# Forty more squared score tiles, 58 pre-added row sums and a tabled instruction order in a two-part attention kernel

## The chip, the cores and the metric

The kernel runs on one core of a Trainium2 chip. The metric is device time in microseconds of one execution; three executions of the kernel before took 1046.61, 1047.0 and 1047.89 us, so their median is 1047.0. The names used below: PE is TensorE (matmuls; its weight loads are shown as PEld), ACT is ScalarE, DVE is VectorE, POOL is GpSimd, SP is SyncE, which here only issues transfers. Line numbers are those of the kernel before unless a line is said to be of the changed one, where the same code lies some 40 to 100 lines further down.

## What is computed

Two attention layers over 2048 tokens of width 1024, with 32 heads of 32 numbers each, whose outputs are laid side by side. Part A is plain softmax attention. Part B cuts the sequence into four segments of 512 tokens, does causal softmax attention inside each, and mixes it with a running memory of the earlier segments.

```python
def _A_ref(x, wqkv, wo):
    qkv = (x @ wqkv).reshape(B, S, 3, H, Dh).transpose(2, 0, 3, 1, 4)
    scores = jnp.einsum('bhqd,bhkd->bhqk', qkv[0], qkv[1]) * Dh ** (-0.5)
    o = jnp.einsum('bhqk,bhkd->bhqd', softmax(scores), qkv[2])
    return o.transpose(0, 2, 1, 3).reshape(B, S, D) @ wo
...
        for s in range(N):                      # part B, segment by segment
            p = _softmax(einsum('bhqd,bhkd->bhqk', qs, ks) * scale + mask)
            a_dot = jnp.einsum('bhqk,bhkd->bhqd', p, vs)
            num = jnp.einsum('bhld,bhde->bhle', phi(qs), M)
            den = jnp.einsum('bhld,bhd->bhl', phi(qs), z)[..., None] + 1e-06
            outs.append(g * num / den + (1.0 - g) * a_dot)
            M = M + jnp.einsum('bhld,bhle->bhde', phi(ks), vs)
            z = z + jnp.einsum('bhld->bhd', phi(ks))
...
    return jnp.concatenate([a, b], axis=-1)
```

## The kernel before

**Tiles and sets.** Heads go in groups of four (`g`, eight groups), queries in chunks of 256 (`c`, eight chunks). A pair `("A", g, c)` is a unit of part A: 64 units. A unit goes over its 2048 keys in eight sets, numbered 0 to 7 by their place in the unit. A set is 256 keys (two key blocks of 128) against the chunk's 256 queries for four heads: four tiles of 128 partitions by 512 columns, one per head, the two key blocks side by side. `plan_set` issues a set's scores as one run of eight matmuls (line 1271, "score row" below) into four PSUM banks. Six banks form three slots of two banks (`SLOT_BANKS`), which the sets use in turn, so that a score row can only go when the exponentials two and three places before it in ACT's stream have emptied their banks. The remaining two banks (`POOL_BANKS`) are shared by the accumulators and all other matmul work. Part B adds 80 sets of the same kind, cut to the causal shape; there are 592 sets in all.

**Exponentials.** For each set ACT runs two instructions (line 1347), each over two tiles: 128x1024, from PSUM to the bf16 tile `P`, a ring of 20 buffers of 512 columns.

**Squared tiles.** In some sets of part A the first of the four tiles isn't exponentiated: DVE writes `Y = a*s + b` (line 1308) and POOL multiplies `Y` by itself into `Pc` (line 1311), a parabola that stands for the exponential of these small scores; a constant that is missing is added through `job_corr` (line 1481) and `cu` (line 1504). The set's first exponential then covers one tile only, 128x512. `SQUARES` names, for each head group, the places in a unit whose sets have such a tile; `Y` has three buffers and `Pc` four. The last two units, ("A", 7, 6) and ("A", 7, 7), and the early units of group 0 have none.

**Products.** `round` (lines 1438 and 1445) does a set's second half: for each of the two key blocks four matmuls of 256 columns with the values `V`, and four with ones, which give the row sums for the softmax. The four matmuls of a group lie in four column strips of the array and run side by side. All of a unit's products add up in one bank; `norm` reads it after the last.

**Jobs.** Everything else (projections at line 899, evictions on DVE at line 1658, output products, memory updates, squares of K and Q at line 1672 that guard the exponential's range) is cut into jobs that are slipped between score rows.

**What sets the order.** The planner makes a list of operations with a duration, a key and due times. `schedule` was a list scheduler: engine by engine it took the ready operation with the best rank, out of constants such as `AHEAD`, `STICK` and `JOB_SLOPE`, and a table `SHIFT` of many hundred numbers moved single operations' keys. After it every engine has a fixed sequence of instructions with waits on the other engines' counters; an engine that waits holds up all that stands behind it.

Of the kernel before, what the change touches and what calls it, by code (L numbers as in the profile page):

```python
# [11 lines left out]
P = 128  # L12
H = 32
DH = 32
S = 2048
# [9 lines left out]
OL_LEAD, OL_MAX = 3.567283411686441, 21.60561264796846  # L25
# [8 lines left out]
SQUARES = ((1, 3, 4, 6, 7), (1, 3, 4, 6, 7), (1, 3, 4, 6), (1, 3, 5, 7), (1, 3, 5, 7), (1, 3, 5, 7), (1, 3, 5, 7), (1, 4, 6))  # L34
HOST = 2
CORR_AT = -0.496
# [3 lines left out]
SOON = 0.5969023125738563  # L40
# [88 lines left out]
class Op:  # L129
# [4 lines left out]
    def __init__(self, eng, fn, dur, lat, key, mode=None, sem=None):  # L134
# [16 lines left out]
SWITCH = 0.1  # L151
WIN = 3.413
ROW_LEAD = 5.053495059459838
AHEAD = 1.6055122421540051
HEAT = 8.05297032017043
STICK = 3.256770423473878
OVER = 17.394741454160474
PV_ROOM = 6.408007584666841
PV_T = 1.0806361081944706
PV_HOT = 1.0883878031673944  # L160
NORM_K = 6.738
JOB_AT = 1.5887710826754966
JOB_SLOPE = 1.1413237083257293
# [3 lines left out]
LEAD_A, LEAD_B, DUE_AT, DUE_SLOPE = 10.658, 3.249, 7.018517831572489, 1.9480960937294671  # L167
HOLD = {}
BACKLOG = 3.378
XR = 70.3728830950375  # L170
XC = 5.80397040345515
# [4 lines left out]
SAFE = 0.0  # L176
SHIFT = {((f, n), e): v for f, e, t in (
# [10 lines left out]
    ("plan_constants", "ACT", {  # L188
        1: 15.5}),
    ("plan_constants", "POOL", {  # L190
        0: 5.5, 2: 4.25, 3: -3, 4: 10.25, 6: -9.5, 7: -0.75, 8: -0.75, 9: 2.25, 11: 3.25, 12: -7, 13: 3.75, 14: -12.25,
        15: 2.5, 16: -0.5, 17: -4.75, 18: 1.5, 19: 3.25, 20: -0.5, 21: 15, 23: 0.75}),
    ("plan_exp", "POOL", {
# [10 lines left out]
    ("plan_jobs", "ACT", {  # L204
# [4 lines left out]
    ("plan_jobs", "DVE", {  # L209
# [91 lines left out]
    ("plan_prologue", "ACT", {  # L301
        4: 6, 5: 3.75, 8: 4, 10: 10}),
    ("plan_prologue", "DVE", {
        0: -2.25, 5: 6, 6: 8.25, 7: -3, 9: -8.5, 10: 0.5}),
    ("plan_prologue", "PE", {
        2: 1.5, 5: -3.25, 6: 12, 7: 5, 8: 17.25, 9: 0.5}),
# [2072 lines left out]
```

## Time and profile before

| | |
|---|---|
| median of three executions | 1047.0 us |
| span of the profiled execution (first to last instruction) | 1044.3 us |
| its own time | only its span is shown; the median is 2.7 us above it |
| granted TensorE clock | 1.000 |
| PE, busy share of the span | 98% |
| ACT | 97% |
| DVE | 67% |
| POOL | 56% |

A matmul's end is modelled and matmuls overlap in the pipeline, so PE's 98% says only that something was under way; how much room PE has is read from what its weight loads wait for, and from the distance between starts. The same holds on ACT, where an instruction begins before the one ahead of it has ended. A row of the groups shows count, busy time, the mean duration of one, the idle time before them and what ended it; a row of the waits shows the time waited in total, how often, and the longest.

### The profile page before, as it was taken

To read this page: it belongs to the slowest core of one execution; us is meant where nothing else is said; L and a number is where in the kernel's file an instruction comes from. 1 tells how busy PE (TensorE), PEld (TensorE's weight loads), DVE (VectorE), ACT (ScalarE), POOL (GpSimd) and SP (SyncE) were. 2 spreads that over 40 slices of the span, in tenths; PEclk is the share of its full clock that TensorE was granted. 3 is DMA by queue.
4 is the path that set the end of the run, shared out by engine and by line. 5 is a ranking of instruction groups with operands and counts; after the bars stand their busy time and mean duration, and the time that the engine had idled before them with its cause. 6 is when DMAs were issued, how large, how long until landed. Compare 5 with 4: busy or idle time off the path is not lost.

```text
span 1044.3 us, 56017 instructions
## 1 busy us (share of the span) xinstructions
PE 1019.2 (98%) x25384; PEld 559.9 (54%) x25385; DVE 700.4 (67%) x1559; ACT 1016.3 (97%) x1225; POOL 585.5 (56%) x677
## 2 busy tenths in 40 slices
PE   8999999999999999999999999999999999999998
PEld 4555555655555555565555545565555545455554
DVE  3366676767566686887865687687755885874444
ACT  5999989999999999999999999999999999999997
POOL 2125476668645675766656476665644775653310
PEclk9999999999999999999999999999999999999999
DMA  9042352124313331033223320133113561021101
GB/s 210 15 96 54 78 130 36 20 38 106 80 42 92 80 79 34 11 99 51 71 58 94 98 60 18 28 92 54 51 29 87 174 171 25 24 79 57 59 24 59
DMA packets 171390, 72.17 MB, mean 69 GB/s; under 512 B 134800, under 2 KB 169360, under 8 KB 171152
## 3 DMA queue, kind: packets, MB, share of 16 engines
q1 hardware_dynamic: 168784, 67.79, 26.7%
q8 instruction: 200, 3.28, 1.3%
q10 hardware_dynamic: 2368, 0.79, 0.3%
q14 instruction: 38, 0.31, 0.1%
HBM read 45.29 MB, written 11.73 MB: 55 GB/s over the span
## 4 chain that ended last, share of the span: by engine, by line
PE 66%; ACT 29%; DVE 3%; issue 1%; DMA 1%; POOL 0%; ACTq 0%; DVEq 0%
PE ps L899 32%; ACT P L1347 28%; PE ps L1271 13%; PE ps L1438 9%; PE ps L1445 9%; PE ps L1964 1%; DMA xT_A<-in_A_x_dram 1%; ACT PKQ_B L2008 1%; DVE Y L1308 1%; DVE T L1508 0%; PE ps L1715 0%; DVE OT_B L2035 0%; DVE T L1510 0%; DVE KQ_B L1658 0%; PE ps L1814 0%
## 5 line engine op out<-in xcount | busy, mean ns | idle before, releaser
L1347 ACT ACTIVATE P<-ps 128x1024 bf16<-128x1024 f32 (+1 forms) x1176 | 988.4, 1059 | 9.8 <-PE ps L1271 3.2
L1311 POOL TENSOR_TENSOR Pc<-Y 128x512 bf16<-128x512 f32 x238 | 249.4, 1049 | 257.2 <-PE ps L899 79.3
L1445 PE MATMUL ps<-P,onesb 128*32 128x256 bf16 (+1 forms) x4388 | 295.9, 270 | 0.8 <-issue 0.7
L1438 PE MATMUL ps<-P,V_A 128*32 128x256 bf16 x3620 | 252.7, 274 | 0.4 <-DVE V_A L1974 0.3
L1308 DVE TENSOR_SCALAR Y<-ps 128x512 f32<-128x512 f32 x238 | 163.4, 686 | 97.7 <-PE ps L1271 83.8
L1271 PE MATMUL ps<-KQ_A 32*128 32x256 bf16 x4096 | 204.0, 273 | 7.4 <-ACT P L1347 5.7
L1271 PEld LDWEIGHTS ps<-KQ_A 32*128 32x128 bf16 x4096 | 62.0, 92 | 154.0 <-ACT P L1347 111.7
L1445 PEld LDWEIGHTS ps<-P,onesb 128*32 128x32 bf16 x4388 | 128.8, 96 | 25.9 <-issue 12.9
L899 PE MATMUL ps<-xT_A,W_A 128*32 128x512 bf16 (+1 forms) x2236 | 138.8, 363 | 2.3 <-DMA xT_A<-in_A_x_dram 1.2
L899 PE MATMUL ps<-xT_B,W_B 128*32 128x512 bf16 (+1 forms) x2284 | 139.0, 359 | 1.2 <-DVE KQ_B L1658 0.3
L1438 PEld LDWEIGHTS ps<-P,V_A 128*32 128x32 bf16 x3620 | 107.7, 96 | 26.2 <-issue 10.9
L1438 PE MATMUL ps<-Pc,V_A 128*32 128x256 bf16 x476 | 119.5, 273 | 0.2
L1445 PE MATMUL ps<-Pc,onesb 128*32 128x256 bf16 x476 | 119.6, 274 | 0.0
L1370 POOL TENSOR_SCALAR_AFFINE_SELECT P<-P 128x768 bf16<-128x768 bf16 (+1 forms) x96 | 75.7, 794 | 49.9 <-ACT P L1347 48.3
L1672 POOL TENSOR_TENSOR sqA<-KQ_A 128x512 bf16<-128x512 bf16 x61 | 64.0, 1061 | 60.9 <-PE ps L899 31.5
L1672 POOL TENSOR_TENSOR sqB<-KQ_B 128x512 bf16<-128x512 bf16 x64 | 68.4, 1070 | 24.9 <-DVE KQ_B L1658 19.0
L899 PEld LDWEIGHTS ps<-xT_B,W_B 128*32 128x32 bf16 x2284 | 53.2, 96 | 46.6 <-issue 17.1
L899 PEld LDWEIGHTS ps<-xT_A,W_A 128*32 128x32 bf16 x2236 | 52.0, 96 | 48.7 <-issue 17.1
L1521 DVE STREAM_TRANSPOSE T<-rc 128x256 f32<-128x256 f32 (+1 forms) x152 | 72.3, 479 | 2.6
L899 PE MATMUL ps<-Wv_B,xT_B 128*32 128x512 bf16 (+1 forms) x1124 | 71.0, 362 | 0.8 <-issue 0.7
L1658 DVE CAST KQ_B<-ps 128x512 bf16<-128x512 f32 x64 | 44.1, 688 | 39.1 <-PE ps L899 38.4
L899 PE MATMUL ps<-Wo_B,OT_B 128*32 128x512 bf16 (+1 forms) x1112 | 68.6, 364 | 0.3 <-DVE T L1504 0.2
(117 smaller groups left out, 1224.5 us busy)
## 6 DMA issues: line engine op xcount, KB each, us to landing
Wv_B<-in_B_wv_dram SPq DMA_DIRECT2D x32, 256.0 KB, 3.3
W_B<-in_B_wk_dram SPq DMA_DIRECT2D x32, 256.0 KB, 3.4
W_B<-in_B_wq_dram SPq DMA_DIRECT2D x32, 256.0 KB, 4.0
Wo_B<-in_B_wo_dram SPq DMA_DIRECT2D x32, 256.0 KB, 3.3
out_dram<-outsb SPq DMA_DIRECT2D x56, 128.0 KB, 1.9
W_A<-in_A_wqkv_dram SPq DMA_DIRECT2D x14, 256.0 KB, 3.4
ot_a_scratch<-OTst SPq DMA_DIRECT2D x51, 64.0 KB, 1.8
xT_A<-ot_a_scratch SPq DMA_DIRECT2D x6, 512.0 KB, 4.9
```

Source lines behind the costliest of these rows:

```text
L899: ins = e.matmul(out[r], w[:, r], x, start=start, stop=stop, tile_position=(0, 32 * t), skip_group_check=True)
L1271: ins = e.matmul(out, kap, qap, start=st, stop=True, tile_position=(32 * h, 0), skip_group_check=True)
L1308: o = self.dve(lambda e: e.tensor_scalar(Y[:, :], src, KAPPA * SCALE, BETA, ALU.mult, ALU.add), 512, key - 9.0, [self.bank[bank]], [rY], f ...
L1311: last.append(self.pool(lambda e: e.tensor_tensor(dst, Y[:, :], Y[:, :], ALU.mult), 512, key - BCK, [rY], [rP], rate=0.56))
L1347: a = self.act(guarded if early else lambda e: e.activation(dst, src, ACT.Exp, scale=SCALE), cols, key, rd, wr, fixed=EXP_FIXED + (0.095 i ...
L1370: self.pool(lambda e: e.affine_select(v, v, pattern=pat, compare_op=ALU.is_ge, fill=0.0, base=0, channel_multiplier=-1), 2 * nd * P, key + ...
L1438: ins = e.matmul(self.pb(obk, q0, q0 + nq, slice(32 * h, 32 * h + 32)), v, p, start=first, stop=last, tile_position=(0, 32 * h), skip_grou ...
L1445: ins = e.matmul(self.pb(obk, QC + q0, QC + q0 + nq, slice(32 * h, 32 * h + 32)), self.onesb[:, 0:32], p, start=False, stop=last, tile_pos ...
L1521: self.dve(lambda e: e.transpose(L2.rearrange("p (b r) -> p b r", r=32), bc), n, key, [rr], [rl], fixed=0.17)
L1658: self.dve(lambda e: e.tensor_copy(dst, src()), 512, key, [self.at(b)], rdst, fixed=0.155)
L1672: self.pool(lambda e: e.tensor_tensor(sq[:, :], src, src, ALU.mult), 512, key, [rsrc], [rs], rate=0.56)
L1964: o = self.pe(lambda e, i=i, t=t, k=k: e.matmul(self.pb(b, P * k, P * k + P), self.xT[:, i, P * t:P * t + P], self.WAv[:, i, P * half:P * ...
```

## The change

It has three parts, and two smaller ones.

First, `SQUARES` gives the places 1, 3, 4, 6, 7 to the head groups 2 to 6 too, which had four of them. That is one more squared tile in each of 40 units: 278 tiles where there were 238.

Second, in 58 units of part A one set that has no squared tile gets its row sums in another way (`ADDED`, `plan_add`, `sums`). POOL adds the set's two key blocks for all four heads into a tile `S` (one instruction, 128x1024 bf16 out of twice as many), and four matmuls with ones take `S`, in place of the eight that took the two blocks. `S` has one buffer.

Third, the list scheduler's choice is gone. `ORDER` holds, for each engine, runs of operations by their place in the planner's list, and `schedule` replays them; the constants of the ranks and `SHIFT` are gone with it.

The smaller ones: `load_xB` brings a segment of part B's input in four transposing transfers of 128x2x512 in place of one of 128x8x512, so 16 in place of 4 over the program; and `BACKLOG`, which spaces out transfers, is 1.2 in place of 3.378.

```diff
-SQUARES = ((1, 3, 4, 6, 7), (1, 3, 4, 6, 7), (1, 3, 4, 6), (1, 3, 5, 7), (1, 3, 5, 7), (1, 3, 5, 7), (1, 3, 5, 7), (1, 4, 6))
+SQUARES = ((1, 3, 4, 6, 7), (1, 3, 4, 6, 7), (1, 3, 4, 6, 7), (1, 3, 4, 6, 7), (1, 3, 4, 6, 7), (1, 3, 4, 6, 7), (1, 3, 4, 6, 7), (1, 4, 6))
+ADDED = (((0, 2, 5), 1, 'POOL'), ((0, 2, 5), 1, 'POOL'), ... ((0, 2, 3, 5, 7), 1, 'POOL'))
+S_RING = 1
+ADDED_PV = 5.0
-BACKLOG = 3.378
+BACKLOG = 1.2
-SHIFT = {((f, n), e): v for f, e, t in (
...
+ORDER = {
...
+        queue = {}
+        for e, runs in ORDER.items():
+            at, q = 0, []
+            for jump, n in zip(runs[::2], runs[1::2]):
+                at += jump
+                q += self.ops[at:at + n]
+                at += n
...
+    def plan_add(self, take, buf, eng, T):
+        i = self.nS % S_RING
+        self.nS += 1
+        rS = self.r_S[i]
+        take[0]["S"] = (i, rS)
+
+        def f(key):
+            lo, hi = self.Pt[:, buf:buf + 4, 0:QC], self.Pt[:, buf:buf + 4, QC:2 * QC]
+            fn = lambda e: e.tensor_tensor(self.S[:, i, :, :], lo, hi, ALU.add)
...
+                self.pool(fn, 4 * QC, key, self.r_P[buf:buf + 4], [rS], rate=0.56)
...
+    def sums(self, t, n, take, key):
+        ob = t["ol"]
+        i, rS = take[0]["S"]
+
+        def mm(e):
+            for h in range(4):
+                ins = e.matmul(self.pb(ob.grp, QC, 2 * QC, slice(32 * h, 32 * h + 32)), self.onesb[:, 0:32], self.S[:, i, h, :],
+                               start=False, stop=True, tile_position=(0, 32 * h), skip_group_check=True)
...
-            for mm in (mm_o, mm_l):
+            for mm in (mm_o, mm_l) if "S" not in parts[0][0][0] else (mm_o,):
...
-        self.turn(self.xTB[:, :, :], xb[L * s:L * s + L, :], self.sm_xTB, key, [], [self.r_xTB], 5.0, 3.4, True)
+        self.pieces(key, X_STEP, [lambda e, i=i: e.dma_start(self.xTB[:, i:i + 2, :], src[:, P * i:P * i + 2 * P], transpose=True)
+                                  for i in range(0, 8, 2)], self.sm_xTB, [self.r_xTB], ("x", s), 3.4, issue=1.25, svc=2.0)
```

What this moves is shown at three places, before and after each. The first is ACT's sequence in the middle of the program (head group 3), where `128x1024` is an exponential of two tiles and `128x512` one beside a squared tile. Before:

```order
L1347 ACTIVATE P<-ps 128x1024 x3
L1347 ACTIVATE P<-ps 128x512
L1347 ACTIVATE P<-ps 128x1024 x3
L1347 ACTIVATE P<-ps 128x512
L1347 ACTIVATE P<-ps 128x1024 x3
```

and now:

```order
L1424 ACTIVATE P<-ps 128x1024 x3
L1424 ACTIVATE P<-ps 128x512
L1424 ACTIVATE P<-ps 128x1024
L1424 ACTIVATE P<-ps 128x512
L1424 ACTIVATE P<-ps 128x1024 x3
```

Every second set had a short exponential; now two neighbouring sets have one, then one set has none.

The second place is PE at the first products of a unit of head group 3: `KQ_A` is a score row, `P,V_A` and `P,onesb` are the products of a key block of four heads with values and with ones, `Pc` is the squared tile among them, `Wv_A,xT_A` a projection, `S` the added blocks. Before:

```order
L1445 MATMUL ps<-P,onesb 32x256 x4
L1438 MATMUL ps<-Pc,V_A 32x256
L1438 MATMUL ps<-P,V_A 32x256 x3
L1445 MATMUL ps<-Pc,onesb 32x256
L1445 MATMUL ps<-P,onesb 32x256 x3
L1271 MATMUL ps<-KQ_A 128x256 x8
```

and now, in the changed kernel's line numbers:

```order
L937 MATMUL ps<-Wv_A,xT_A 32x256 x40
L1534 MATMUL ps<-P,V_A 32x256 x12
L1541 MATMUL ps<-P,onesb 32x256 x4
L1346 MATMUL ps<-KQ_A 128x256 x8
L1534 MATMUL ps<-P,V_A 32x256 x4
L1541 MATMUL ps<-P,onesb 32x256 x4
```

Twelve products with values now stand in a row where a product with ones stood between each two: the two products with ones of the added set are gone there. They come back as one group, after the score row that follows:

```order
L1541 MATMUL ps<-Pc,onesb 32x256
L1541 MATMUL ps<-P,onesb 32x256 x3
L1495 MATMUL ps<-S,onesb 32x256 x4
L1534 MATMUL ps<-Pc,V_A 32x256
L1534 MATMUL ps<-P,V_A 32x256 x3
```

The third place is POOL, just behind a memory update of part B (`Mb`), where squares of scores (`Pc`), squares of K and Q (`sqA`) and a unit's scaled output (`OTst`) follow one another. Before:

```order
L2075 TENSOR_TENSOR Mb<-Mf,maskbd 128x256
L1672 TENSOR_TENSOR sqA<-KQ_A 128x512
L1311 TENSOR_TENSOR Pc<-Y 128x512 x3
L1570 TENSOR_TENSOR OTst<-T_0 128x256
L1311 TENSOR_TENSOR Pc<-Y 128x512 x2
```

and now:

```order
L2171 TENSOR_TENSOR Mb<-Mf,maskbd 128x256
L1288 TENSOR_TENSOR S<-P 128x1024
L1388 TENSOR_TENSOR Pc<-Y 128x512 x2
L1680 TENSOR_TENSOR T_1<-T_1 128x256
L1681 TENSOR_TENSOR OT_B<-T_1,OT_B 128x256
```

The add of a whole set stands ahead of squares, which POOL takes up only when it is done.

More of the change, by code (lines that the diff above doesn't have):

```diff
@@ L509, in schedule @@
     def schedule(self):
-        pend = {}
-        groups = list(dict.fromkeys(o.grp for o in self.ops if o.grp is not None))
-        for g in groups:
-            own = {*g.pe, *g.rd}
-            first = g.pe[0]
-            g.left = len(g.pe)
-            if g.chain:
-                continue
-            first.gate = [(x, 0.0) for o in g.pe[1:] for x in (o.deps | o.order) - own]
-            first.gate += [(x, sum(o.dur for o in g.pe)) for o in g.rd for x in (o.deps | o.order) - own]
-            assert g.rd and not any(x.grp is g and x not in own for x in first.deps)
@@ L549, in schedule @@
+        for q in queue.values():
+            for n, o in enumerate(q):
+                o.pos = n
+        for o in self.ops:
+            assert all(x.eng != o.eng or x.pos < o.pos for x in o.order)
+        at = dict.fromkeys(queue, 0)
+        free = dict.fromkeys(queue, 0.0)
+        ready = dict.fromkeys(queue)
         last = {b: list(r.w) + list(r.r) for b, r in self.before.items()}
         holder = dict.fromkeys(last)
-        st = self.st = dict(mode=None, prog=0.0, act_end=0.0, recent=[], win=0, acts={}, slow=0.0, opn=0, dma=0.0,
-                            rows=sum(o.urgent is not None and o.eng == "PE" for o in self.ops))
+        acts, win, low, mode, held, dma = {}, 0, False, None, 0.0, 0.0
@@ L554, in ready_of @@
+        done = set()
+        progs, was_pe = [], None
+        for g in dict.fromkeys(o.grp for o in self.ops if o.grp is not None):
+            g.left = len(g.pe)
         def ready_of(o):
             t = 0.0
-            job = SAFE if o.eng == "PE" and o.urgent is None else 0.0
+            for x in o.deps | o.order:
+                if x not in done:
+                    return None
             for x in o.deps:
-                t = max(t, x.end + (SELF if x.eng == o.eng and x.sem is None else x.lat) + (job if x.eng in ("DVE", "POOL") else 0.0) +
+                t = max(t, x.end + (SELF if x.eng == o.eng and x.sem is None else x.lat) +
@@ L559, in ready_of @@
                         (TO_POOL if o.eng == "POOL" and x.eng == "DVE" else 0.0) +
                         (TO_DVE if o.eng == "DVE" and x.eng == "PE" else 0.0))
-            for x in o.order:
-                t = max(t, x.start)
-            for x, w in o.gate:
-                t = max(t, x.end + x.lat - w)
-            return t
-        def past(t):
-            return next((x for x in reversed(queue["ACT"]) if x.prog and x.end <= t), None)
-        def opens(o):
-            return o.grp is not None and o is o.grp.pe[0]
@@ L574, in opening @@
-        def opening(o, now=False):
-            g = o.grp
-            if g.sums and ((g.prev is not None and (g.prev.left or not all(x.sched for x in g.prev.rd))) or st["opn"] < g.at and st["rows"] and not now):
-                return 1e9, None
-            return min((1e9 if holder[b] is not None and holder[b].left else
-                        max((x.end + x.lat + SAFE if x.sched else 1e9 for x in last[b]), default=0.0), b) for b in last)
-        def heat(t, span):
-            r = st["recent"]
-            while r and r[0][1] < t - 4.0:
-                r.pop(0)
-            return sum((min(e, t) - max(s, t - span)) * w for s, e, w in r if e > t - span)
@@ L635, in schedule, with opening @@
+            return max([t] + [x.start for x in o.order])
+        def opening(b):
+            if holder[b] is not None and holder[b].left or not done.issuperset(last[b]):
+                return 1e9
+            return max((x.end + x.lat for x in last[b]), default=0.0)
+        left = len(self.ops)
         while left:
             best = None
-            for e, c in cand.items():
-                if c:
-                    t = max(free[e], min(x.ready for x in c))
-                    if best is None or t < best[0]:
-                        best = (t, e)
@@ new lines, in schedule @@
+            for e, q in queue.items():
+                if at[e] == len(q):
+                    continue
+                o = q[at[e]]
+                if ready[e] is None:
+                    ready[e] = ready_of(o)
+                    if ready[e] is None:
+                        continue
+                t, b = max(free[e], ready[e]), None
+                if o.grp is not None and o is o.grp.pe[0]:
+                    v, b = min((opening(b), b) for b in last)
+                    if v >= 1e9:
+                        continue
+                    t = max(t, v)
+                if e == "SP" and o.svc >= 0.8:
+                    t = max(t, dma - BACKLOG)
+                if best is None or t < best[0]:
+                    best = (t, e, o, b)
@@ L1009, in alloc @@
         self.p_n = 0
+        self.S = sb("S", [P, S_RING, 4, QC])
+        self.r_S = [Res() for _ in range(S_RING)]
+        self.nS = 0
+        self.nadd = {}
         self.Y = [sb(f"Y{i}", [P, 512], dt.float32) for i in range(Y_RING)]
@@ L1224, in squared, with added @@
         return SQUARES[unit[1]]
+    def added(self, unit, part, at):
+        if unit[0] != "A" or part is not None or unit in WHOLE:
+            return None
+        ats, most, eng = ADDED[unit[1]]
+        if at not in ats or self.nadd.get(unit, 0) == most or self.p_n % P_RING + 4 > P_RING:
+            return None
+        self.nadd[unit] = self.nadd.get(unit, 0) + 1
+        return eng
+    def plan_add(self, take, buf, eng, T):
[6 more added lines that the diff above has]
+            fn = lambda e: e.tensor_tensor(self.S[:, i, :, :], lo, hi, ALU.add)
+            if eng == "DVE":
+                self.dve(fn, 4 * QC, key, self.r_P[buf:buf + 4], [rS], rate=1.92, fixed=0.155, port=True)
+            else:
+                self.pool(fn, 4 * QC, key, self.r_P[buf:buf + 4], [rS], rate=0.56)
+        self.item(T + 0.05, f, take[0]["set"])
     def plan_set(self, take, T):
@@ L1234, in plan_set @@
         cube = kind == "A" and at in self.squared(take[0]["unit"], take[0]["part"])
-        bufs = [self.p_next(2 - (cube and not k)) for k in range(2)]
+        add = self.added(take[0]["unit"], take[0]["part"], at) if kind == "A" else None
+        assert add is None or not cube
+        if add is not None:
+            bufs = [self.p_next(4)]
+            bufs.append(bufs[0] + 2)
+        else:
+            bufs = [self.p_next(2 - (cube and not k)) for k in range(2)]
         for k, t in enumerate(take):
@@ L1284, in plan_set @@
             T += (2 - lo) * w / 1200.0 + EXP_FIXED
+        if add is not None:
+            self.plan_add(take, bufs[0], add, T)
         u = take[0]["unit"]
```

239 lines of the change are left out of this document (60 added, 179 removed), and 673 rows, old and new, of tables (ORDER, SHIFT).

## The prediction

> **What bounds the kernel now.** I read the page first, then who waits for whom, then the gaps between starts, then the stretches of the program.
>
> ```profile
> span 1044.3 us, 56017 instructions
> PE 1019.2 (98%) x25384; PEld 559.9 (54%) x25385; DVE 700.4 (67%) x1559; ACT 1016.3 (97%) x1225; POOL 585.5 (56%) x677
> PEclk9999999999999999999999999999999999999999
> ```
>
> Two engines look full and two have room; the clock is granted in full throughout, so no time is to be had there. Which of the two full ones leads is told by the waits of all engines; a row has waiter, what it waits for, total, times, longest:
>
> ```profile
> PEld ps L1271 <- ACT P L1347: 133.8, 416, 1.5
> PEld ps L1271 <- DVE Y L1308: 21.5, 67, 0.6
> PEld ps L1271 <- issue: 14.7, 62, 0.4
> ACT P L1347 <- PE ps L1271: 3.2, 8, 0.9
> ```
>
> PE's score rows wait for exponentials 416 times; ACT is seen waiting for score rows 8 times. So ACT leads. How much room does PE have? A row that waits for nothing still shows about 0.24 us (14.7 over 62, "issue"); the timeline around such a row shows 0.21 us between the last group ahead and the row:
>
> ```profile
> 500.03 0.27 PE L1445 MATMUL ps<-Pc,onesb 128*32 128x256 bf16 x1
> 500.14 0.27 PE L1438 MATMUL ps<-Pc,V_A 128*32 128x256 bf16 x1
> 500.25 0.27 PE L1445 MATMUL ps<-Pc,onesb 128*32 128x256 bf16 x1
> 500.46 0.40 PE L1271 MATMUL ps<-KQ_A 32*128 32x256 bf16 x8
> ```
>
> Taking 0.21 off each of the 416 + 67 waits leaves 155.3 - 101.4 = 54 us: PE's true room is some 54 us, 5% of the span, not the 2% of the page.
>
> ACT isn't as full as it looks either. Its instructions overlap, so a late one hides inside the duration of its neighbour.
>
> ```profile
> L1347 ACT ACTIVATE P<-ps 128x1024 bf16<-128x1024 f32 x938 | 922.7, 1147 | 9.3 <-PE ps L1271 3.0 <-PE ps L899 2.9 <-PE ps L1445 1.5
> L1347 ACT ACTIVATE P<-ps 128x512 bf16<-128x512 f32 x238 | 169.5, 712 | 0.5 <-PE ps L1271 0.2
> L2008 ACT ACTIVATE PKQ_B<-KQ_B 128x1024 bf16<-128x1024 bf16 x16 | 19.1, 1196 | 0.0
> 14.21 8.15 ACT L1334 ACTIVATE P<-ps,bias 128x1024 bf16<-128x1024 f32 x8 [2.06 <-DVE bias L1776]
> 499.87 8.97 ACT L1347 ACTIVATE P<-ps 128x1024 bf16<-128x1024 f32 x10
> 534.73 56.84 ACT P L1347 x71
> L1347 ACT ACTIVATE P<-ps 128x1024 bf16<-128x1024 f32 x53 | 55.0, 1264 | 0.0
> 1028.87 7.69 ACT L1347 ACTIVATE P<-ps 128x1024 bf16<-128x1024 f32 x8
> ```
>
> Ten long ones in 8.97 us are 0.90 us each (the fifth row). The chain of waits has a stretch of 56.84 us that is ACT alone: 71 exponentials, 53 of them long (the group of that stretch), 18 short, so a short one takes (56.84 - 53 x 0.90) / 18 = 0.51 us. All of them at that pace: 946 x 0.90 + 238 x 0.51 = 973 us. With the 16 long and 16 short activations of line 2008 at the same pace, 23 us, it is 996 us. They run from 14.2 to 1028.87 + 7.69 = 1036.6, or 1022 us. ACT loses 26 us to late rows, PE has 54 us of room: ACT leads, PE is close behind, and each set is settled between them.
>
> **The change part by part.** *Squared tiles.* 40 exponentials become short. Each saves 0.90 - 0.51 = 0.39 us by the stretch, 1147 - 712 = 435 ns by the two means: 15.6 to 17.4 us off the engine that leads; I take 0.42, 16.8 us. On DVE come 40 x 0.686 = 27.4 us, on POOL 40 x 1.05 = 42 us (rows next). On PE their products only change names (`P` to `Pc`), and ten tiny matmuls of `job_corr` are added, under 1 us.
>
> ```profile
> L1308 DVE TENSOR_SCALAR Y<-ps 128x512 f32<-128x512 f32 x238 | 163.4, 686 | 97.7 <-PE ps L1271 83.8 <-ACT P L1347 6.1 <-PE ps L899 3.3
> L1311 POOL TENSOR_TENSOR Pc<-Y 128x512 bf16<-128x512 f32 x238 | 249.4, 1049 | 257.2 <-PE ps L899 79.3 <-DVE Y L1308 76.2 <-PE ps L1438 34.1
> L1672 POOL TENSOR_TENSOR sqA<-KQ_A 128x512 bf16<-128x512 bf16 x61 | 64.0, 1061 | 60.9 <-PE ps L899 31.5 <-DVE KQ_A L1658 11.6 <-PE ps L1715 7.1
> L1570 POOL TENSOR_TENSOR OTst<-T 128x256 bf16<-128x256 f32 x47 | 34.6, 736 | 14.6 <-DVE T L1521 13.5 <-DVE cu L1464 1.0
>   PEld ps L1438: 0.2, 1
> ```
>
> *Added sums.* PE loses 58 groups of four matmuls of 256 columns; groups start 0.11 us apart (the timeline above), so 6.4 us, 6.0 with `job_corr`. The add itself has no row. Its nearest is `sqA`, half as wide with both inputs in bf16: twice 1.061 is 2.1 us; by the slope from `OTst` (256 columns, 0.736) to `sqA` it is 1.06 + 2 x 0.325 = 1.7. I take 2.0, being nearer to `sqA`: 58 x 2.0 = 116 us on POOL, between 99 and 123. POOL comes to 585.5 + 42 + 116 = 744 us, DVE to 728, each some 71% of the new span: no engine's total is the bound. What covers the adds is POOL's idle time, and the distance to their reader: in the order, `S` is used five to seven score rows behind the row of its own set, 8 us or more, against 2. The last row above, from the view of tile `Pc`, says how well POOL's latency is covered now: in the whole run PE waited once, 0.2 us, for a squared tile. Without that cover each add costs up to its 2.0 us.
>
> *The table.* It moves every instruction, so I ask whether each stretch has the room to take ACT's gain. The waits of score rows for exponentials in the six stretches of 100 us from 245 to 845, which hold almost all of the 40 units:
>
> ```profile
> PEld ps L1271 <- ACT P L1347: 13.2, 44, 0.4
> PEld ps L1271 <- ACT P L1347: 13.2, 39, 0.7
> PEld ps L1271 <- ACT P L1347: 11.9, 41, 0.5
> PEld ps L1271 <- ACT P L1347: 16.9, 47, 1.5
> PEld ps L1271 <- ACT P L1347: 12.8, 37, 1.1
> PEld ps L1271 <- ACT P L1347: 13.4, 41, 0.9
> ```
>
> Less 0.21 us each: 4.0, 5.0, 3.3, 7.0, 5.0 and 4.8, or 29 us in 600. ACT wants to be 16.8 us shorter there, PE gives back 40 x 0.11 = 4.4, so PE's room falls to 29 - 16.8 + 4.4 = 17 us, from 4.8% to 2.8%. It doesn't run out, hence most of ACT's gain should arrive; but rows that fall late by chance do so more often with less room, and each costs ACT directly. Bounds: all of it, 16.8; or only what PE gives up, 6.0. I take three quarters, 12.6 us, and 0.4 us more from the 18 added sums outside these stretches, where PE's room hides most: 13 us. A table that also closes gaps gains up to the 26 us which ACT loses today; one that opens them costs as much. I have no row for either and count the table itself as zero.
>
> *Transfers.* Four transposes of `xT_B` took 3.8 to 5.1 us of SP's time each; sixteen shorter ones free SP's queue in between for others. Nothing on PE or ACT waits for them in the view of that tile:
>
> ```profile
> L1623 SPq DMA_TRANSPOSE xT_B<-in_B_x_dram x4: 3795/4295/5070, 52.7 to 682.0; - x4
> ```
>
> So 0; if all 16 had to be waited for at a quarter of 5 us, 20 us, which the time between their issue and first use would have to shrink by first.
>
> **The sum.** 1044.3 - 12.6 - 0.4 = 1031.3 us of span. The median lies 2.7 us above the profiled span, so 1034.0.
>
> **The rivals.** *ACT's gain in full, or more.* For it: ACT leads in every stretch above, and the sum of room stays positive. Against: room falls by two fifths. It gives 1047.0 - 16.8 = 1030; with half of the 26 us lost to late rows closed by the table, 1017. *PE takes over.* For it: 54 us of room is an average, and PE shows 100.0 busy of 100 in the stretch from 245 (below). Then only PE's saving counts: 1047.0 - 6.0 = 1041.
>
> ```profile
> 245.00:345.00 100.00, 99.98 (x2496) 54.21 (x2484) 62.12 (x129) 98.84 (x122) 59.47 (x64) 1.00 0.28 72
> 845.00:945.00 100.00, 96.68 (x2354) 50.36 (x2357) 73.91 (x174) 99.39 (x119) 59.77 (x72) 1.00 0.19 51
> ```
>
> *POOL's queue holds the score row (slower).* The place: an add stands ahead of squares in POOL's sequence. It needs all four tiles of its set, so it waits through two exponentials and then runs 2.0 us; the squares behind it keep `Y` buffers, of which there are three; DVE's next `Y` then waits, and with it the bank that the next score row needs. For it: rows already wait 67 times for `Y`, and two neighbouring squared sets now follow each other every 1.4 us (0.90 + 0.51). Against: the single wait of 0.2 us for `Pc`, and a unit's POOL work, 5 x 1.05 + 2.0 + 0.74 + 1.06 = 9.1 us, is less than the 12.5 us which its exponentials take (3 sets of 1.8 and 5 of 1.41). It decides from 13 / 58 = 0.22 us of delay per added set; at 0.5 us, it costs 29 us: 1047.0 - 13 + 29 = 1063. *DVE is held by POOL (no change).* Some of DVE's instructions stretch when POOL is at work:
>
> ```profile
> L2014 DVE SCALAR_TENSOR_TENSOR PKQ_B<-KQ_B,PKQ_B x48: 644/728/1528, 114.4 to 920.3; 128x512 bf16<-128x512 bf16 x48
> L2010 DVE TENSOR_SCALAR PKQ_B<-PKQ_B x32: 239/418/1256, 114.1 to 919.5; 128x512 bf16<-128x512 bf16 x16, 128x1024 bf16<-128x1024 bf16 x16
> L2026 DVE TENSOR_SCALAR Zb<-maskbd,zf x24: 183/458/1064, 115.3 to 901.9; 128x128 bf16<-128x128 bf16 x24
> ```
>
> The longest are 0.9 to 1.0 us over the shortest, the length of one POOL square. With adds of 2.0 us the longest would be 2 us over. If each of these 104 lost a tenth of a microsecond more and all of it reached ACT, 10 us would go: 1044 to 1047. The Trainium skill ("SBUF — State Buffer", section "Who interferes with whom") states that GpSimd and VectorE share one port pair as an exclusive lock, held for the whole instruction by whichever starts first, for VectorE's two-port modes and its instructions with two SBUF inputs. The maxima above agree with it, and it speaks against a POOL instruction of double length. What no run here shows is how often an add would be the holder.
>
> **How the numbers follow.** Forecast, 1031.5 to 1038: 0.42. ACT's gain in full or more, below 1031.5: 0.27, of which 0.08 below 1022. PE takes over, 1038 to 1044.9: 0.13. DVE held, or a table that eats the gain, within 0.2% of 1047.0 (1044.9 to 1049.1; a measurement of this kernel can't tell less from no change): 0.06. POOL's queue, above 1049.1: 0.12. So faster 0.82, same 0.06, slower 0.12. The range leaves out the 0.08 below 1022 and, above 1046, about 0.14.
>
> **What would show it.** Right: 898 long and 278 short exponentials of line 1424, with the same 0.90 and 0.51 us between starts; ACT still the engine that score rows wait for, but PE's net wait down from 54 us to 35 to 50; 58 adds of 1.7 to 2.1 us; waits of PE for `Pc` and `S` under 3 us in total. Wrong towards faster: ACT's loss to late rows well below 26 us. Wrong towards slower: rows of POOL or `Y` among the large waits of score rows, `ACT P <- PE ps` grown to tens of microseconds, an add of over 3 us, or PE waiting for `S`.

## The result and the profile after

The changed kernel took 1039.18 us (median of four executions, 1038.53 to 1039.97), the kernel before 1046.80: 0.9924 of it, 95% interval 0.9907 to 0.9942, or 7.6 us less. It is faster and inside the range; of the 13 us that the sum promised, 58% came. It missed the forecast's own band (1031.5 to 1038) and lies in the band that the prediction had given, with a chance of 0.13, to the second rival (1041, "PE takes over"), so the mechanism needs testing, not only the number.

The page of the profiled execution: span, busy times, granted clock, shares of the chain by engine.

```profile
span 1036.8 us, 55738 instructions
PE 1012.1 (98%) x25123; PEld 552.1 (53%) x25123; DVE 725.8 (70%) x1599; ACT 1004.6 (97%) x1225; POOL 745.8 (72%) x775
PEclk9999999999999999999999999999999999999999
PE 60%; ACT 12%; DVE 5%; issue 1%; POOL 1%; DVEq 0%; ACTq 0%; POOLq 0%
```

The totals of DVE and POOL came out as forecast (728 and 744). ACT's share of the chain of waits was 29% before:

```profile
PE 66%; ACT 29%; DVE 3%; issue 1%; DMA 1%; POOL 0%; ACTq 0%; DVEq 0%
```

The chain of the changed kernel could be followed back only to 221 us, so its shares add up to 79% of the span. Of what was followed, ACT has 15% here and 23% in a second profile of the same kernel (`c_same`, below), so this share is too unsteady to tell by itself who leads.

Now the waits of the changed kernel (waiter, what it waits for, total, times, longest):

```profile
PEld ps L1346 <- ACT P L1424: 116.1, 360, 1.0
PEld ps L1346 <- DVE Y L1385: 28.3, 77, 1.4
PEld ps L1346 <- issue: 26.0, 99, 0.4
ACT P L1424 <- PE ps L1346: 6.9, 15, 1.4
```

Less the 0.21 us that every such wait costs, score rows wait 40.5 us for exponentials (46.4 before) and 12.1 us for `Y` (7.4 before). The first became smaller, the second larger, and the two together hardly moved: 52.6 us, against 53.9. ACT waits for score rows twice as often.

The groups of the exponentials, of `Y` and of the adds, different shapes apart (count | busy, mean ns | idle time before them and what ended it):

```profile
L1424 ACT ACTIVATE P<-ps 128x1024 bf16<-128x1024 f32 x898 | 887.6, 1125 | 6.4 <-PE ps L1346 2.4 <-DVE cu L1560 1.8 <-POOL sqB L1768 0.3
L1424 ACT ACTIVATE P<-ps 128x512 bf16<-128x512 f32 x278 | 190.8, 686 | 5.8 <-PE ps L1346 4.5 <-PE ps L1541 0.3
L1385 DVE TENSOR_SCALAR Y<-ps 128x512 f32<-128x512 f32 x278 | 191.3, 688 | 101.9 <-PE ps L1346 77.5 <-ACT P L1424 12.1 <-POOL T L1680 2.9
L1288 POOL TENSOR_TENSOR S<-P 128x1024 bf16<-128x1024 bf16 x58 | 124.0, 2138 | 26.5 <-ACT P L1424 20.1 <-PE ps L1534 3.4 <-PE ps L937 1.6
```

How much of its saving did ACT keep? Its timeline gives the first and the last exponentials, and the chain one stretch of ACT alone:

```profile
14.12 2.12 ACT L1411 ACTIVATE P<-ps,bias 128x1024 bf16<-128x1024 f32 x2 [2.06 <-DVE bias L1872]
225.02 13.57 ACT P L1424 x15
1009.64 18.02 ACT L1424 ACTIVATE P<-ps 128x512 bf16<-128x512 f32 x20
```

The pace is as before: 13.57 / 15 = 0.905 us, the 0.90 of a long one. So the 906 long ones (eight of them of line 1411) need 815 us, the 278 short ones at 0.51 us 142 us, and with the 23 us of the other activations it is 980. They run from 14.1 to 1027.7, 1013.5 us: ACT now loses 33 us to late rows, where it lost 26. Its work fell by 16 us, its stream by 9.

### The profile page after: what moved, and what is told of

Its sections match the earlier page's. It is cut to its first block, busy times and chain, and to the rows that moved or that the text cites. A ratio compares the mean times of both kernels' runs of the same rounds, so it can differ in the third digit from the quotient of the medians.

```text
span 1036.8 us, 55738 instructions
## 1 busy us (share of the span) xinstructions
PE 1012.1 (98%) x25123; PEld 552.1 (53%) x25123; DVE 725.8 (70%) x1599; ACT 1004.6 (97%) x1225; POOL 745.8 (72%) x775
## 4 chain that ended last, share of the span: by engine, by line
PE 60%; ACT 12%; DVE 5%; issue 1%; POOL 1%; DVEq 0%; ACTq 0%; POOLq 0%
PE ps L937 30%; PE ps L1346 12%; ACT P L1424 12%; PE ps L1534 9%; PE ps L1541 8%; DVE Y L1385 1%; DVE T L1604 1%; PE ps L1495 1%; PE ps L1811 0%; DVE T L1617 0%; DVE T L1606 0%; DVE PKQ_B L2106 0%; DVE PKQ_B L2110 0%; DVE Zb L2122 0%; POOL P L1448 0%
## 5 line engine op out<-in xcount | busy, mean ns | idle before, releaser
L1424 ACT ACTIVATE P<-ps 128x1024 bf16<-128x1024 f32 (+1 forms) x1176 | 975.1, 1021 | 12.2 <-PE ps L1346 6.9
L1388 POOL TENSOR_TENSOR Pc<-Y 128x512 bf16<-128x512 f32 x278 | 290.9, 1058 | 106.4 <-DVE Y L1385 32.3
L1541 PE MATMUL ps<-P,onesb 128*32 128x256 bf16 (+1 forms) x3844 | 269.1, 270 | 0.0
L1385 DVE TENSOR_SCALAR Y<-ps 128x512 f32<-128x512 f32 x278 | 191.3, 688 | 101.9 <-PE ps L1346 77.5
L1534 PE MATMUL ps<-P,V_A 128*32 128x256 bf16 x3540 | 244.6, 274 | 0.8 <-DVE cols L1866 0.2
L1288 POOL TENSOR_TENSOR S<-P 128x1024 bf16<-128x1024 bf16 x58 | 124.0, 2138 | 26.5 <-ACT P L1424 20.1
L1541 PE MATMUL ps<-Pc,onesb 128*32 128x256 bf16 x556 | 139.5, 274 | 0.5 <-issue 0.5
L1534 PE MATMUL ps<-Pc,V_A 128*32 128x256 bf16 x556 | 139.6, 274 | 0.1
L1541 PEld LDWEIGHTS ps<-P,onesb 128*32 128x32 bf16 x3844 | 115.6, 96 | 15.6 <-issue 7.9
L1534 PEld LDWEIGHTS ps<-P,V_A 128*32 128x32 bf16 x3540 | 104.9, 96 | 24.1 <-issue 9.7
L1768 POOL TENSOR_TENSOR sqB<-KQ_B 128x512 bf16<-128x512 bf16 x64 | 67.7, 1065 | 14.9 <-DVE KQ_B L1754 12.6
```

What stands on the lines that cost most here:

```text
L1288: fn = lambda e: e.tensor_tensor(self.S[:, i, :, :], lo, hi, ALU.add)
L1385: o = self.dve(lambda e: e.tensor_scalar(Y[:, :], src, KAPPA * SCALE, BETA, ALU.mult, ALU.add), 512, key - 9.0, [self.bank[bank]], [rY], f ...
L1388: last.append(self.pool(lambda e: e.tensor_tensor(dst, Y[:, :], Y[:, :], ALU.mult), 512, key - BCK, [rY], [rP], rate=0.56))
L1424: a = self.act(guarded if early else lambda e: e.activation(dst, src, ACT.Exp, scale=SCALE), cols, key, rd, wr, fixed=EXP_FIXED + (0.095 i ...
L1534: ins = e.matmul(self.pb(obk, q0, q0 + nq, slice(32 * h, 32 * h + 32)), v, p, start=first, stop=last, tile_position=(0, 32 * h), skip_grou ...
L1541: ins = e.matmul(self.pb(obk, QC + q0, QC + q0 + nq, slice(32 * h, 32 * h + 32)), self.onesb[:, 0:32], p, start=False, stop=last, tile_pos ...
```

## The experiments

Three theories were to be told apart. One: ACT led and PE stood close behind, as the prediction says, so the missing 5 us went to PE's side. Two: the adds in POOL's queue ate them. Three: something that the sum had left at nothing ate them. All cuts and undoings below keep the changed kernel's table of order, only without the operations that are gone, so that no other instruction changes places; cuts in the kernel before keep its own order in the same way. Each was timed beside the kernel before; where kernels of different comparisons are set against each other, their ratios are used. The uncut changed kernel has two, 0.9924 and (`c_same`, below) 0.9943, mean 0.9934.

**The parts undone, one at a time.** First the added sums out, with the products with ones back behind the products with values:

```diff
-        if unit[0] != "A" or part is not None or unit in WHOLE:
-            return None
+        return None                             # in added()
```

> The changed kernel without the 58 added sums: their 58 adds are gone from POOL, the 58 groups with S are gone from PE, and the two products with ones of each of those sets stand right behind the product with V of their key block; everything else in the tabled order is left as it is. PE gets 58 x 0.11 = 6.4 us more, POOL 124 us less. If ACT leads (the forecast's reading): 1 to 2 us slower than the changed kernel, 1040 to 1041. If PE has taken over as the bound (rival): the full 6.4 us, about 1045.6. If POOL's adds hold score rows (the slower rival, hidden under a gain): faster, below 1038.

Measured: 1040.11 us, 0.9946 (0.9932 to 0.9960). That is about 0.001 above the mean of the uncut one, 1 us, with intervals that overlap. Its POOL is busy 120 us less and its PE 6 us more than the changed kernel's, and DVE, with the same 1599 instructions, is busy 9 us less:

```profile
PE 1017.8 (98%) x25347; PEld 560.2 (54%) x25347; DVE 716.8 (69%) x1599; ACT 1006.5 (97%) x1225; POOL 625.8 (60%) x717
PEld ps L1338 <- ACT P L1416: 109.3, 326, 1.1
PEld ps L1338 <- DVE Y L1377: 26.9, 78, 0.6
```

So the added sums as a whole bring next to nothing. This run takes a saving (PE's 6 us) and a burden (the adds on POOL, and what they do to DVE) away together, so it can't tell two small amounts from a larger gain and a larger loss that cancel. The waits for `Y` are there without the adds too.

Then the 40 squared tiles out, adds and table kept; head groups 2 to 6 have their squares at the places 1, 3, 6, 7. The constant that the squared tiles need in the row sums stays as for five of them, one number without a price in time.

```diff
+        real = cube and at in OLD[take[0]["unit"][1]]    # OLD: (1, 3, 6, 7) in groups 2 to 6
+        take[0]["real"] = real
-            if cube and not k:
+            if real and not k:
```

> The changed kernel without the 40 additional squared tiles: the head groups 2 to 6 have them at the places 1, 3, 6, 7 alone, so 238 in all; the tile at place 4 goes back to ACT, whose exponential is long again, and its DVE and POOL instructions are gone. Adds and tabled order stay. ACT gets 40 x 0.42 = 16.8 us more, DVE 27 and POOL 42 us less. If ACT leads: 12.6 to 16.8 us slower than the changed kernel, 1052 to 1056. If PE has taken over: 0 to 2 us, about 1040. If neither leads and each set is settled between them: about half, 1047.

And both out, with the table kept:

> Both undone: 238 squared tiles, no adds, so the work of the kernel before (the squares at other places, 1, 3, 6, 7), in the order of the table. This shows the table alone. If the table is worth nothing, as the forecast counted it: 1047 plus or minus 2. If it opened gaps that ate part of the gain: 1050 to 1056. If it closes gaps, so that the two parts brought next to nothing: 1040 to 1044.

Measured: 1060.85 us, 1.0149 (1.0134 to 1.0165) without the squares; 1058.5 us, 1.0122 (1.0107 to 1.0138) without both. The waits of score rows for exponentials, of the first:

```profile
PEld ps L1345 <- ACT P L1427: 156.2, 432, 1.2
```

and of the second, where the changed kernel has 116.1 us in 360:

```profile
PEld ps L1334 <- ACT P L1416: 149.3, 404, 1.2
```

Without the squares the kernel is 22 us slower than the changed one, more than the 16 us that they take off ACT. With both out the kernel does the amount of work of before (with squares at other places) in the changed kernel's order, and it is 13 us slower than before. Both times lie above every outcome named in advance: an order is fitted to its work. An undoing in a fitted order therefore prices a part together with the misfit that it leaves, and can't split the 7.6 us. What it does show: in this order nothing of the gain is left without the squares, and the table can't be given a number apart from the work it was made for.

**Small cuts at a fixed order.** Cuts of some 13 us from one engine, so small that the order still fits, ask what each engine's time is worth. Off ACT: 36 of 1024 columns left out of the long exponentials of head groups 2 to 6 (440 in the changed kernel).

```diff
-                src = self.ps[:, c0:c0 + cols]
-                dst = Pt.rearrange("p b n -> p (b n)")
+                src = self.ps[:, c0:c0 + cols - cut]
+                dst = Pt.rearrange("p b n -> p (b n)")[:, 0:cols - cut]
```

> The changed kernel with 36 of the 1024 columns left out of each long exponential of part A in the head groups 2 to 6 (these columns keep older values, so the output isn't the reference's). About 440 instructions lose 36 / 1.2 = 30 ns each by the step from 0.90 to 0.51 us for half the columns (28 ns): some 12.5 us off ACT, nothing off any other engine, same order. If ACT leads: 9 to 12 us faster than the changed kernel, 1027 to 1030. If PE has taken over: 0 to 2 us, 1037 to 1039. If they are coupled: about half, 1033.

> The kernel before with the same cut in its long exponentials of the head groups 2 to 6 (480 or so, 13.5 us off ACT; same columns left out as in the changed kernel's case). The forecast let three quarters of ACT's saving through: 10 us faster than before, 1037. If the kernel before was already coupled: 5 to 7 us, 1040 to 1042. Much more than in the changed kernel's case would mean that the lead passed from ACT to PE with the change.

Off PE: the products with ones of the second key block over half the queries, same head groups.

```diff
+                    if half:                # second key block, groups 2 to 6
+                        nq, p = nq // 2, p[:, 0:nq // 2]
```

> The changed kernel with the products with ones of every second key block in the head groups 2 to 6 over half the queries, 128 in place of 256 columns (the other half of these row sums is left out, so the output isn't the reference's). 280 groups start 47 ns sooner (0.109 to 0.062): some 13 us off PE, nothing off any other engine, same order. If ACT leads: 0 to 2 us faster than the changed kernel. If PE has taken over: 10 to 13 us, 1026 to 1029. If they are coupled: about half, 1033.

> The kernel before with the same cut in the products with ones (320 groups, 15 us off PE). The forecast held that PE's saving hides while ACT leads: 0 to 2 us faster than before. If already coupled: 5 to 8 us.

| cut | kernel before | changed kernel |
|---|---|---|
| ACT, some 13 us | 1042.67 us, 0.9970 (0.9959 to 0.9981): 3 us | 1036.05 us, 0.9914 (0.9901 to 0.9928): 0.0020 under the uncut, 2 us |
| PE, 13 to 15 us | 1043.94 us, 0.9987 (0.9978 to 0.9996): 1.5 us | 1033.89 us, 0.9889 (0.9874 to 0.9905): 0.0045 under, 5 us |

Before, the cut on ACT gave twice as much as the one on PE; now the one on PE gives twice as much as the one on ACT. The intervals of each pair still overlap a little, so the order is clearer than the factor, but the lead did pass to PE. No cut returns much over a third, though. Above all, ACT's time was worth far less before than the forecast held: of the 13.5 us 3 arrived, where three quarters would have been 10 and even the lower case named 5 to 7. And the changed kernel's chain with the cut on PE, followed over 79% of the span, shows no engine alone:

```profile
PE 43%; ACT 27%; DVE 5%; issue 2%; POOL 2%; DVEq 0%; ACTq 0%; POOLq 0%
```

**Both cuts, and the other two engines.** Four kernels of one comparison: the changed kernel itself, both cuts at once, and one cut each on DVE and POOL.

> The changed kernel once more, unedited, so that the three cuts of this comparison have it beside them. All theories: 1039, 0.7 to 0.8% below the kernel before. If it comes out more than 2 us away, the earlier comparisons with it shift by as much.

> The changed kernel with both cuts at once: in groups 2 to 6, 36 columns less in some 440 long exponentials (12.5 us off ACT) and half the queries in the products with ones of the second key block (13 us off PE). Alone they gave about 3 us (ACT) and 5 us (PE). Theory A, the two engines are coupled and nothing else bounds: each cut alone is stopped by the other engine, so together they give more than the sum of both, 10 to 13 us, 1026 to 1029. Theory B, what is left in these stretches is set by the order's stalls or by a third engine (DVE's Y, POOL): together no more than the sum, 5 to 8 us, 1031 to 1034. Left out of the computation: the last 36 columns of those exponentials, and half the row sums of those blocks.

> The changed kernel, with Y of the squared tiles in groups 2 to 6 over 256 of 512 columns: some 0.27 us off each of 200, 53 us off DVE, and the bank of the next score row free sooner where Y is the last reader. Score rows wait 77 times for Y in the changed kernel, 28.3 us in sum and 12 us net of 0.21 us each. Theory A (only PE and ACT bound): within 1.5 us of the changed kernel, 1037.5 to 1040.5. Theory B (DVE's Y is the third party that took the missing gain): 4 to 10 us less, 1029 to 1035. Left out: half of the columns of those squared tiles.

```diff
-            src = self.ps[:, 512 * bank:512 * bank + 512]
-            o = self.dve(lambda e: e.tensor_scalar(Y[:, :], src, ...
+            n = 256 if 2 <= t["g"] <= 6 else 512
+            src = self.ps[:, 512 * bank:512 * bank + n]
+            o = self.dve(lambda e: e.tensor_scalar(Y[:, 0:n], src, ...
```

> The changed kernel, with all added sums but the first over 128 of 256 queries: about 1 us off each of 57 adds, 57 us off POOL, all of it in POOL's queue ahead of squares. Theory A (POOL is covered): within 1.5 us of the changed kernel, 1037.5 to 1040.5. Theory B (the prediction's third rival in a small dose: an add holds the squares, these hold Y, and Y holds the bank of a score row): if the delay per add is 0.1 us, 5 to 6 us less, 1033 to 1034. Left out: the added sums of half the queries.

```diff
-            fn = lambda e: e.tensor_tensor(self.S[:, i, :, :], lo, hi, ALU.add)
+            n = QC // 2 if self.added_once else QC
+            fn = lambda e: e.tensor_tensor(self.S[:, i, :, 0:n], lo[:, :, 0:n], hi[:, :, 0:n], ALU.add)
```

| kernel | us | ratio (interval) | under the uncut |
|---|---|---|---|
| uncut | 1039.96 | 0.9943 (0.9929 to 0.9956) | |
| ACT and PE cut | 1029.60 | 0.9846 (0.9832 to 0.9859) | 10.4 us |
| DVE's `Y` cut | 1034.28 | 0.9885 (0.9870 to 0.9900) | 5.7 us |
| POOL's adds cut | 1037.61 | 0.9925 (0.9911 to 0.9938) | 2.3 us, intervals overlap |

Set against one and the same uncut ratio, the mean 0.9934, the two cuts together give 9 us where alone they give 2 and 5. That speaks for PE and ACT being coupled, but a surplus of 2 us isn't clear of intervals of some 1.4 us to either side. And 10.4 us of 25, at 1029.60, falls between what was named for two engines alone (1026 to 1029) and for a third party (1031 to 1034). The cut on `Y` takes 47 us off DVE (725.4 to 678.2 us busy) and gives 5.7 us, about as much as 13 us off PE, from an engine that is busy 70%. The cut on the adds takes 54 us off POOL (745.6 to 691.2) and gives about 2, if anything: 0.04 us per add for half an add.

**Was `Y` there before?** One more run tells whether the change brought it: the same cut in the kernel before.

> The kernel before with the same cut on DVE: Y of the squared tiles of groups 2 to 6 over 256 of 512 columns (some 0.27 us off each). In the changed kernel this cut gave 5 to 6 us (ratio 0.9885 beside 0.9943 for the uncut one). Theory A, the change brought the wait for Y (rows' waits for Y net of 0.21 us each: 7.4 us before, 12.1 after): here the cut gives clearly less, 0 to 3 us, 1043 to 1046. Theory B, Y held the score rows before the change just as much: 5 us or more, 1040 to 1041. Left out: half of the columns of those squared tiles.

Measured: 1045.33 us, 0.9998 (0.9989 to 1.0007): nothing. The waits of score rows from 245 to 845 us, for exponentials and for `Y`, are in the kernel before, uncut and then cut:

```profile
PEld ps L1271 <- ACT P L1347: 81.6, 249, 1.5
PEld ps L1271 <- DVE Y L1308: 12.8, 40, 0.6
```

```profile
PEld ps L1271 <- ACT P L1348: 83.4, 257, 1.5
PEld ps L1271 <- DVE Y L1309: 2.7, 7, 0.6
```

and the changed kernel, uncut and then cut:

```profile
PEld ps L1346 <- ACT P L1424: 60.6, 183, 0.8
PEld ps L1346 <- DVE Y L1385: 20.8, 54, 1.4
```

```profile
PEld ps L1346 <- ACT P L1425: 65.6, 199, 0.7
PEld ps L1346 <- DVE Y L1386: 6.3, 13, 1.0
```

In both kernels the cut takes most of the waits for `Y` away: net of 0.21 us each, 4.4 to 1.2 us before and 9.5 to 3.6 us after. It is tempting to set the 5.9 us of waits beside the 5.7 us of time. But a row that no longer waits for `Y` may wait for something else. The idle time of PE's weight loads ahead of all score rows of part A, with what ended most of it, is for the changed kernel, uncut and then cut:

```profile
L1346 PEld LDWEIGHTS ps<-KQ_A 32*128 32x128 bf16 x4096 | 62.0, 92 | 158.6 <-ACT P L1424 99.2
L1346 PEld LDWEIGHTS ps<-KQ_A 32*128 32x128 bf16 x4096 | 61.9, 92 | 158.6 <-ACT P L1425 100.8
```

The sum is the same (and 154.0 and 153.6 us in the kernel before). Of it, `Y` ended 26.5 us uncut and 12.3 us cut, while the part in which a row waits for nothing that the profile shows ("issue") went from 22.8 to 32.2 us. PE's fixed order is the same in both, so the distances between the starts of its weight loads can be compared one by one: ahead of score rows they shrink by 0.2 us in all, out of the 3.6 us by which the two profiles differ. The rest came out ahead of other matmuls: 0.8 us at a transfer in the beginning that landed sooner, and most of the remainder where PE had waited for other results of DVE or had stood still on "issue". Three rows of the waits that shrank, uncut and then cut:

```profile
PEld ps L937 <- issue: 64.3, 291, 1.8
PEld ps L937 <- DVE T L1604: 3.4, 12, 0.6
PEld ps L1534 <- DVE OT_B L2131: 2.1, 5, 1.0
```

```profile
PEld ps L937 <- issue: 62.9, 289, 1.3
PEld ps L937 <- DVE T L1605: 1.7, 7, 0.4
PEld ps L1535 <- DVE OT_B L2132: 1.3, 4, 0.5
```

So one thing is shown: time on DVE has a price in the changed kernel (5.7 us for 47) and had none before, where the cut took 38 us off DVE (700.4 to 662.8) for nothing. That the wait of score rows for `Y` is the place where it is paid isn't shown, and the rows above speak against it; a DVE whose queue moves on sooner is the likelier reading. Two profiles of the uncut changed kernel already differ by 1.4 us of span (1036.8 and 1038.2), with some 2.5 us more of stops on "issue" in the longer one, so one profile each can't settle where the 5.7 us lie. Whether the forty more `Y`, the adds or the table brought DVE into play stays open too.

## Why the prediction was right, and where its size was off

The time fell inside the range because the range held the bands of two rivals as well; the forecast's own band missed it.

*What bounds the kernel.* That ACT led, with PE close behind, holds: before, a cut on ACT gave twice what one on PE gave. "Each set is settled between them" holds for before, where a shorter `Y` changed nothing. It isn't the whole of the changed kernel, where time on DVE has a price too.

*Squared tiles, off ACT 16.8 us.* Right: 898 long and 278 short exponentials, 16 us less work. The shortest distance to the next start, in both traces, is 0.904 us behind a long one and 0.48 us behind a short one, not 0.51; with that ACT's loss to late rows is some 30 us before and 38 after in place of 26 and 33, and the difference stays.

*The three quarters.* This is the step that failed: the term was mis-sized, and so was the reasoning behind it, that a leading engine whose followers have room keeps most of a saving. Forecast: 12.6 of 16.8 us arrive. In ACT's own stream 9 of 16 arrived, and 7.6 in the result. The cut on ACT in the kernel before shows that this isn't owed to the change alone: there, in that kernel's own order, only 3 of 13.5 us arrived. What holds the rest back is in part the coupling with PE (both cuts at once gave 9 to 10 us of 25); the remainder stays open. The forecast's room for PE in the stretches, 29 us falling to 17, was wrong too: net waits for exponentials there fell to 22.2 us, and those for `Y` rose to 9.5, together 31.7 against 33.7. The sign of it was named ("PE's net wait down from 54 us to 35 to 50"), and it didn't come: 52.6.

*"No engine's total is the bound."* True as it stands, but the sum drew from it that DVE costs nothing, and that failed as well. DVE's total was forecast within 3 us, and a total of 70% isn't a bound. Yet in the changed kernel 47 us off DVE returned 5.7 us. The row `PEld ps L1271 <- DVE Y L1308: 21.5, 67` stood in the prediction as a third thing that rows wait for, and a large row of `Y` was named as a sign of wrong towards slower; it grew from 7.4 to 12.1 us net. It was counted into PE's room, and the sum had no term for DVE. That this row is where DVE's time is paid isn't shown.

*Added sums.* Right in size: an add took 2.14 us by its group (124.0 over 58; forecast 2.0, bounds 1.7 to 2.1, so just above the upper), PE lost 6 us, and PE waited for `S` twice, 0.4 us in all. What they bring as a whole, 1 us at this order by the run without them, can't be told from nothing.

*The table, counted as zero.* Not to be measured by itself: for the work of before, the new order is 13 us worse than the old one, and for the new work no other order was run.

*The rivals.* ACT's gain in full: false, 1030 or less wasn't reached. PE takes over: its time (1041) is the nearest. What is true of it is that PE's time is now worth more than ACT's. But if PE alone decided, 13 us off PE would have given nearer 13 than 5, and a cut on DVE next to nothing. (The run without the adds, 1 us slower and not 6, is no test of it: it freed POOL and DVE as well.) POOL's queue: 0.04 us for half an add, so perhaps twice that for a whole one, against the 0.22 at which it would decide. DVE held by POOL: it happens, and at one place it can be seen in full. Timeline of the changed kernel (start, length, engine, what; idle time and its releaser in brackets):

```profile
439.79 2.14 POOL L1288 TENSOR_TENSOR S<-P 128x1024 bf16<-128x1024 bf16 x1
439.92 2.29 DVE L2106 TENSOR_SCALAR PKQ_B<-PKQ_B 128x1024 bf16<-128x1024 bf16 x1
442.13 0.68 DVE L1754 CAST KQ_A<-ps 128x512 bf16<-128x512 f32 x1
442.73 0.68 DVE L1385 TENSOR_SCALAR Y<-ps 128x512 f32<-128x512 f32 x1
443.46 0.12 PEld L1346 LDWEIGHTS ps<-KQ_A 32*128 32x128 bf16 x8 [1.39 <-DVE Y L1385]
443.91 0.60 ACT L1424 ACTIVATE P<-ps 128x512 bf16<-128x512 f32 x1 [1.09 <-PE ps L1346]
```

An add starts, a DVE instruction that starts 0.13 us later ends with it, the eviction and `Y` queue behind, the score row waits 1.39 us for `Y`, and ACT stands 1.09 us. With the adds halved the same pair shrinks together, and without an add the DVE instruction takes 0.42 us:

```profile
440.60 1.16 POOL L1291 TENSOR_TENSOR S<-P 128x512 bf16<-128x512 bf16 x1
440.73 1.32 DVE L2109 TENSOR_SCALAR PKQ_B<-PKQ_B 128x1024 bf16<-128x1024 bf16 x1
443.29 0.12 PEld L1349 LDWEIGHTS ps<-KQ_A 32*128 32x128 bf16 x8 [0.42 <-DVE Y L1388]
```

```profile
441.79 0.42 DVE L2098 TENSOR_SCALAR PKQ_B<-PKQ_B 128x1024 bf16<-128x1024 bf16 x1
```

That is the 2 us over the shortest which the rival named. But ACT stands some 1 us here, not 10, and the middle ones of the three groups are no longer than before (min/median/max of the changed kernel; the medians were 728, 418 and 458):

```profile
L2110 DVE SCALAR_TENSOR_TENSOR PKQ_B<-KQ_B,PKQ_B x48: 640/708/1481, 122.9 to 911.1; 128x512 bf16<-128x512 bf16 x48
L2106 DVE TENSOR_SCALAR PKQ_B<-PKQ_B x32: 245/418/2290, 113.0 to 908.3; 128x512 bf16<-128x512 bf16 x16, 128x1024 bf16<-128x1024 bf16 x16
L2122 DVE TENSOR_SCALAR Zb<-maskbd,zf x24: 191/454/1153, 175.5 to 897.0; 128x128 bf16<-128x128 bf16 x24
```

It isn't the only place: over the whole run DVE is busy 9 us longer with the adds than without them (725.8 and 716.8 us, the same 1599 instructions). What those 9 us cost isn't told by any run alone.

The Trainium skill ("SBUF — State Buffer", section "Who interferes with whom") says that one of the two holds the port pair for its whole instruction; the lengths 0.42, 1.32 and 2.29 us beside no add, one of 1.16 and one of 2.14 us agree with it.

## What to carry to other kernels

When work moves from the leading engine to an idle one, the total of the idle engine says little, and the sum needs a term for it: here 47 us off an engine that was busy 70% returned 5.7 us. In an order in which several engines take turns, 13 to 15 us off one full engine bought 1.5 to 5 us. Whether an engine leads doesn't tell what its time is worth; a small cut in the kernel as it stands, at its fixed order, does. Undoing a part also prices the misfit. And when a cut makes one row of waits shrink, look at the whole idle time ahead of the waiter before calling it time won: here the row lost 14 us and the sum nothing.

## What the runs showed of the hardware

Beside the stretched DVE instruction one thing was not expected. In the middle of a run of projection matmuls, behind no wait that the profile shows, PE stood still, and ACT behind it; timeline of the changed kernel:

```profile
708.66 0.84 PE L937 MATMUL ps<-Wv_A,xT_A 128*32 128x256 bf16 x24 [1.63 <-issue]
709.99 0.60 ACT L1424 ACTIVATE P<-ps 128x512 bf16<-128x512 f32 x1 [1.37 <-PE ps L1346]
```

The longest idle time of this kind ahead of a weight load of this line was 1.0 us in the kernel before, 1.8 us in both profiles of the changed kernel, 1.7 us without the squares, 1.3 us with `Y` halved, 1.2 us with the adds halved, 0.9 us without the adds and 0.8 us without both. Its cause is open.
